# Spatial-shift token mixing in a GFNet + S-MLP block: eleven matmuls a block from packed transposes, with two neighbour copies

## The chip, the cores and the metric

The kernel runs on one core of one Trainium2 chip. The metric is the device time of one execution in microseconds (us); the table below gives the median of three runs and, beside it, the one execution that the profiler recorded.

## The reference

x has 2048 tokens of 448 features, w1 and w2 are 448x448, w3 is 448x1792, w4 is 1792x448; all are float32.

```python
x  = A_x;  xn = layernorm(x)
A  = irfft2(rfft2(xn) * (w_r + 1j * w_i))        # global filter branch
h  = gelu(layernorm(xn) @ w1)                    # token mixing of branch B
g0 = shift(h[:, 0:112], +1);   g1 = shift(h[:, 112:224], -1)      # by tokens, zeros at the ends
g2 = shift(h[:, 224:336], +2); g3 = shift(h[:, 336:448], -2)
x1 = xn + concat(g0, g1, g2, g3) @ w2
B  = x1 + gelu(layernorm(x1) @ w3) @ w4          # channel MLP
out = x + A + B
```

The part that the change touches is the token mixing: the product with w2 takes each quarter of h from another token.

## The kernel before, in words

**Precision.** Each float32 operand of a product is kept as two float16 tiles, a high half and a low half (what the high half leaves). A product is three passes: high x high, high x low, low x high. The weights are first scaled by a power of two that comes from their mean square (`squares`, `powers`, lines 238 to 257).

**Blocks of tokens.** Token 16a + b lies on partition a of block b, so the 2048 tokens are 16 blocks of 128 rows (`xb(b)`), and the neighbour of a token is the same partition of the neighbouring block, but for the ends: behind block 15 comes block 0, one partition further. The blocks are worked on in four groups of four, `GRP = [[14,15,0,1],[2,3,4,5],[6,7,8,9],[10,11,12,13]]`.

**First product** (`w1_in`, `w1_unit`, lines 408 to 441). Groups 0 to 2 are normalised, transposed on TensorE and split (L374, L378, L379), group 3 is transposed by DMA (`turn`, L842). Then each block makes eleven matmuls of 448 columns with w1 (L414). The first group's four blocks run side by side, pass by pass, in four PSUM banks. ScalarE applies the gelu in place (L433) and copies the high half (L434), VectorE makes the low half (L435); both lie in one of a few buffers `hs_buf` as 2 halves x 4 quarters x 128 columns (112 used). One DMA transpose a block (L438, on SP's queue) turns that into the eight 112-row tiles of `hT`.

**Token mixing** (`w2_tile`, L443 to L457). For each block b, quarter k is taken from the transposed tile of block b minus 1, plus 1, minus 2 or plus 2; at the ends the offset by one partition is one column of `hT` to the left or right, for which group 0's tiles have extra zero columns. Three passes of each of four quarters: twelve matmuls of 112 rows and 448 columns. VectorE adds the result into x (L456).

**After it.** `ln2` normalises x1, splits it and transposes it by DMA (L490) into `x2all`, which lies in the scratch tile `x2mem`. The channel MLP runs in pairs of blocks G (`front` L385 with w3, gelu and halves at L705 to L708, `back` L787 with w4). Its matmuls fill the gaps of the Fourier branch (L543, L601, L618, L646, L667, L688). w3 is loaded with x at the start (L213), its last part later (L216); the four pieces of w4 are loaded behind the transposes of groups 2 and 3 into `x2mem` (L228) and squared there (L242).

**What sets the order.** The Tile scheduler lays out each engine's instructions when the kernel is built, from the order of the code, priorities (`prio`) and the `behind(...)` marks (an instruction is placed behind another). On the chip each engine runs that list in order. SP issues nearly all DMAs of the kernel, in its own order, on one queue. TensorE begins with `WARM` = 28 matmuls on zeros (L817) while the first inputs are loaded.

Of the kernel before, what the change touches and what calls it, by code (L numbers as in the profile page):

```python
# [25 lines left out]
SHIFT = [1, -1, 2, -2]  # L26
WARM = 28
# [9 lines left out]
HS = 3  # L37
# [31 lines left out]
def constants():  # L69
# [20 lines left out]
    for c in range(NC):  # L90
        for j8, (k1, t) in enumerate(slots(c)):
            for j, (kr, s, base) in enumerate(rows(c)):
                if base != k1:
                    continue
                phi = tau * np.outer(np.arange(NB), kr + 128 * np.arange(16)) / S
# [28 lines left out]
def body(tc, nc, x, wf, w1, w2, w3, w4, c_g, c_n, c_small, out):  # L124
# [46 lines left out]

    def stage(name, n, side, dtype=F32):
        t = pw.tile([128, 1808], F32, tag=f"stage{side}", bufs=1, name=name)
        return (t if dtype is F32 else t.bitcast(dtype))[:, :n]
# [31 lines left out]
    SY.dma_start(w2s[:112], w2.rearrange("(k p) n -> p k n", p=112))  # L206
# [14 lines left out]
    x2mem = pw.tile([128, 9 * F], F16, name="x2mem")  # L221
    x2all = x2mem[:, 0:8 * F].rearrange("p (j t n) -> p j t n", j=4, t=7)
    w4raw = x2mem.bitcast(F32)[:, F:].rearrange("p (f n) -> p f n", f=14)
    w4v = w4.rearrange("(f p) n -> p f n", p=128)
    W4F = (0, 4, 8, 11, 14)

    def load_w4(i):
        SY.dma_start(w4raw[:, W4F[i]:W4F[i + 1]], w4v[:, W4F[i]:W4F[i + 1]])  # L228

    csm = pc.tile([128, 2 * (256 + 2 * DF + 452 + 128)], F16, name="csm")  # L230
# [162 lines left out]
    w2p = pr.tile([112, 2, 4, D], F16, name="w2p")  # L393
# [3 lines left out]

    def h_alloc(g):
        t = {0: 0, 1: 1, 2: 2, 3: 1}[g]
        hT[g] = pr.tile([128, 8, 512 if g else 592], F16, tag=f"h{t}", name=f"h{g}")  # L400
        if g == 0:
            P.memset(hT[g][:, :, 0:576].rearrange("p t (b a) -> p t b a", b=4)[:, :, :, 0:16], 0.0)
            P.memset(hT[g][:, :, 576:592], 0.0)

    def h_at(g, i):
        return 128 * i if g else 144 * i + 16
# [9 lines left out]

    hs_buf = [p1.tile([128, 2, 4, 128], F16, name=f"hs{i}") for i in range(HS)]
    for t in hs_buf:
        P.memset(t.rearrange("p i k n -> p (i k) n")[:, :, 112:], 0.0)

    for o in (0, 1024):
        hs_buf.append(x2mem[:, o:o + 1024].rearrange("p (i k n) -> p i k n", i=2, k=4))
        P.memset(hs_buf[-1].rearrange("p i k n -> p (i k) n")[:, :, 112:], 0.0)

    def w1_unit(g, i, pm=None):
        if pm is None:
            pm = bank(("tr" if g == 1 else "mm", "acc")[i // 2], f"pw1_{g}{i}")
            w1_in(g, [(i, pm)], range(4))
        c = CS[GRP[g][i]]
        pm = pm[:, :D]  # L430
        pv_ = pm.rearrange("p (k n) -> p k n", k=4)
        h = hs_buf[c % (HS if g == 3 else HS + 2)]
        A.activation(out=pm, in_=pm, func=AF.Gelu_apprx_tanh, scale=gsc[:, c:c + 1])  # L433
        u = A.activation(out=h[:, 0, :, 0:112], in_=pv_, func=AF.Copy, scale=h1)  # L434
        v = V.scalar_tensor_tensor(out=h[:, 1, :, 0:112], in0=pv_, scalar=h1, in1=h[:, 0, :, 0:112],  # L435
                                   op0=ALU.mult, op1=ALU.subtract)
        o = h_at(g, i)
        d = SY.dma_start_transpose(out=hT[g][:, :, o:o + 128], in_=h.rearrange("p i k n -> p (i k n)"))  # L438
        after[g, i] = u.ins, v.ins
        after["h", g, i] = (d.ins,)  # L440

    def w2_tile(b):
        pm = bank("sp", f"pw2_{b}")  # L443
        n = 0
        for k in (2, 0, 1, 3):
            src, o = b - SHIFT[k], 1
            if src < 0:
                src, o = src + NB, 0
            elif src >= NB:
                src, o = src - NB, 2  # L450
            g, i = WHERE[src]
            o += h_at(g, i) - 1
            for hi, wi in ((0, 0), (0, 1), (1, 0)):
                T.matmul(pm[:, :D], hT[g][:112, 4 * hi + k, o:o + 128], w2p[:, wi, k], start=n == 0, stop=n == 11)  # L454
                n += 1
        V.scalar_tensor_tensor(out=xb(b), in0=xb(b), scalar=cs[:, CS[b]:CS[b] + 1], in1=pm[:, :D],  # L456
                               op0=ALU.mult, op1=ALU.add)  # L457

    def ln2(bs, engines):
# [22 lines left out]
        for i in range(n):  # L482
# [7 lines left out]
            d = SY.dma_start_transpose(out=x2all[:, b // 4][:, :, 128 * (b % 4):128 * (b % 4) + 128], in_=h)  # L490
            after[f"b{b0}"] = u.ins, v.ins, d.ins

    def unscale(p, part):
        t = part.rearrange("p (b n) -> p b n", b=2)
        SY.dma_start(t, xv[:, 2 * p:2 * p + 2])
        return lambda: V.scalar_tensor_tensor(out=xt[p], in0=xt[p], scalar=p12, in1=t, op0=ALU.mult, op1=ALU.add)

    def finish(b):
        t = xb(b)
        if b < 2:  # L500
            t = row()[:, :D]
            SY.dma_start(t, xv[:, b])
            V.scalar_tensor_tensor(out=t, in0=xb(b), scalar=p12, in1=t, op0=ALU.mult, op1=ALU.add)
        SY.dma_start(ov[:, b], t)
# [6 lines left out]
    def do_fold(b0):  # L511
        X = pfd.tile([128, 2, D + 1], F32, tag="xf", bufs=3, name=f"xf{b0}")
        after["X", b0] = (SY.dma_start(X[:, :, 0:D], xv[:, b0:b0 + 2]).ins,)
# [181 lines left out]
    def front(G, fp, tag):  # L695
        tok = slice(256 * (G % 2), 256 * (G % 2) + 256)
        pm = bank(tag, f"pw3_{G}{fp}")
        for ff in range(2):
            f = 2 * fp + ff
            mlp_in(pm[:, 256 * ff:256 * ff + 256], w3p, slice(128 * f, 128 * f + 128), x2all[:, G // 2], tok)  # L700
# [66 lines left out]
    def back(G, fp):  # L767
# [10 lines left out]
        for i in range(2):  # L778
# [12 lines left out]
            if end:  # L791
                with prio(EVAC):
                    for r, to in parts:
                        V.scalar_tensor_tensor(out=xb(b)[:, r], in0=to, scalar=p34[:, min(G, 1):min(G, 1) + 1],  # L794
                                               in1=xb(b)[:, r], op0=ALU.mult, op1=ALU.add)
                        if G > 4:
                            SY.dma_start(ov[:, b, r], xb(b)[:, r])
# [51 lines left out]
    def w4_split(f):  # L849
        split_w(w4p[0][:, 0, f:f + 2], w4p[0][:, 1, f:f + 2], w4raw[:, f:f + 2], s4)  # L850
# [7 lines left out]
    h_alloc(0)  # L858
# [8 lines left out]
    for t in range(4):  # L867
        w1_in(0, list(enumerate(first)), [t])
    n1[0][0]()
    with behind("w1", 1):  # L870
        n1.append(norm1(1, [P, V, A, V]))
    with behind("w1", 3):
        squares(m2[:112], flat(w2s[:112]))
# [10 lines left out]
    n1[1][0]()  # L884
    with behind("a1"):
        w1_unit(0, 0, first[0])
        n1.append(norm1(2, [P, V, A, P]))
    with behind("a1"), behind("n", 2):
        for k in range(1, 4):
            w1_unit(0, k, first[k])  # L890
    with behind("na", 2):
        for k in range(4):
            split_w(w2p[:, 0, k], w2p[:, 1, k], w2s[:112, k], s2[:112], P)
    h_alloc(1)
# [3 lines left out]
    with behind("h", 1, 3):  # L898
        load_w3([3])
    n1[2][0]()  # L900
# [4 lines left out]
    h_alloc(2)  # L905
    for k in range(4):
        w1_unit(2, k)
    for k in range(4):
        with behind(*(("a2",), ("a2",), (2, 0), (2, 1))[k]):
            squares(m3[:, k:k + 1], w3raw[:, k])  # L910
    s3, r3 = powers(m3, 4, "3", "mm")
# [8 lines left out]
    with behind("t", 3), behind("h", 2, 3), behind("b0"):  # L920
        for i in range(4):
            load_w4(i)
    for b in range(4, 8):
        w2_tile(b)
        with behind(*PIN[b - 4]):
            w3_split(2 * b - 8)
            w3_split(2 * b - 7)
            for i in (2 * b - 10, 2 * b - 9):
                if i >= 0:
                    squares(m4[:, i:i + 1], flat(w4raw[:, 2 * i:2 * i + 2]), junk4)  # L930
    squares(m4[:, 6:7], flat(w4raw[:, 12:14]), junk4)
    ln2([2, 3], [A, P])
    h_alloc(3)
# [11 lines left out]
    for j in range(4):  # L945
        homes[j] = x2mem[:, F * j:F * j + F]
# [122 lines left out]
```

## Time and profile before

| | us |
|---|---|
| median of three runs (410.96 to 412.3) | 411.34 |
| the profiled execution, whole | 410.65 |
| its span, first to last instruction | 408.9 |
| TensorE matmuls busy in the span | 402.3 (98%) |
| VectorE busy | 330.7 (81%) |
| ScalarE busy | 256.5 (63%) |
| GpSimd busy | 95.3 (23%) |
| hardware DMA queue, share of 16 engines | 46.0% |

The durations and places used later are those of the profiled execution, counted from the start of its span. PE is TensorE's matmul, PEld its weight load, DVE VectorE, ACT ScalarE, POOL GpSimd, SP the engine that issues the DMAs. A line number (L454) is a line of the kernel before.

### The profile page before, as it was taken

The page shows a single profiled execution, that of the slowest core. Times are in us where ns is not written, and L with a number is a line of the kernel's source. Part 1 is how long each engine was busy: PE and PEld are TensorE (multiplying, and loading weights), DVE is VectorE, ACT ScalarE, POOL GpSimd, SP SyncE. Part 2 cuts the span into 40 slices and gives each one's busy share as a digit, 9 for nine tenths or more (in the row PEclk, how much of TensorE's full clock was granted, in tenths as well). Part 3 has the DMA queues.
Part 4 walks back from the last instruction along what each step waited for, and adds up shares of the span by engine and source line. Part 5 has one row for each costly group of instructions (what it writes and reads, how often), then busy time and mean ns, then how long its engine had stood idle before and what let it go on. Part 6 is the DMA issues. An engine that isn't in the chain of part 4 may idle for free.

```text
span 408.9 us, 8745 instructions
## 1 busy us (share of the span) xinstructions
PE 402.3 (98%) x3409; PEld 299.0 (73%) x3409; DVE 330.7 (81%) x686; ACT 256.5 (63%) x434; POOL 95.3 (23%) x172
## 2 busy tenths in 40 slices
PE   7999999999999999999999999999999999999996
PEld 3655555765668777777887887877777779998995
DVE  4888999898857678887798888955899989966645
ACT  4698879973758866556598888863453554453431
POOL 3877720101336748400012111110000000000000
PEclk9999999999999999999999999999999999999999
DMA  8959879914786456516255666500011022100101
GB/s 278 354 192 179 153 149 321 177 62 90 156 231 202 137 196 210 170 59 183 63 145 143 155 156 171 147 27 3 24 68 69 25 88 85 55 2 2 45 2 45
DMA packets 56168, 51.28 MB, mean 125 GB/s; under 512 B 37632, under 2 KB 50496, under 8 KB 56128
## 3 DMA queue, kind: packets, MB, share of 16 engines
q1 hardware_dynamic: 56128, 50.74, 46.0%
q8 instruction: 26, 0.43, 0.4%
q14 instruction: 14, 0.11, 0.1%
HBM read 38.28 MB, written 3.67 MB: 103 GB/s over the span
## 4 chain that ended last, share of the span: by engine, by line
PE 94%; DVE 3%; DMA 2%; POOL 0%; issue 0%; ACT 0%; SPq 0%; POOLq 0%
PE pw L385 33%; PE acc L787 23%; PE pw L454 9%; PE pw L414 6%; PE side L757 4%; PE acc L757 3%; PE pu L646 3%; PE ps L543 3%; PE pe L667 2%; PE pp L601 2%; PE px L618 2%; PE py L688 2%; DVE sta L293 1%; DMA xt<-x 1%; DMA h<-hs 1%; PE pta L374 1%
## 5 line engine op out<-in xcount | busy, mean ns | idle before, releaser
L385 PE MATMUL pw<-x2mem,w3p 128*128 128x256 f16 x1232 | 151.1, 273 | 0.0
L385 PEld LDWEIGHTS <-w3p 128*128 128x128 f16 x1232 | 119.2, 98 | 20.6
L787 PE MATMUL acc<-w4p,hf 128*128 128x448 f16 (+1 forms) x516 | 105.4, 348 | 0.0
L787 PEld LDWEIGHTS <-hf 128*128 128x128 f16 x516 | 49.8, 98 | 36.5
L705 ACT ACTIVATE pw<-pw,pe 128x512 f32<-128x512 f32 x42 | 27.5, 655 | 35.7 <-PE pw L385 35.7
L708 DVE SCALAR_TENSOR_TENSOR hf<-pw,h,hf 128x512 f16<-128x512 f32 x42 | 31.3, 748 | 14.5 <-ACT hf L707 14.4
L454 PE MATMUL pw<-w2p,h 112*128 112x448 f16 x192 | 39.9, 352 | 0.8 <-DMA h<-hs 0.8
L414 PE MATMUL pw<-w1p,xT 128*128 128x448 f16 x176 | 35.4, 352 | 0.0
L627 POOL TENSOR_TENSOR z<-te 128x450 f32<-128x450 f32 x16 | 15.7, 982 | 70.3 <-DVE te L625 70.3
L454 PEld LDWEIGHTS <-h 112*128 112x128 f16 x192 | 18.6, 98 | 17.2 <-DMA h<-hs 1.0
L707 ACT ACTIVATE hf<-pw,h 128x512 f16<-128x512 f32 x42 | 28.7, 686 | 1.0
L414 PEld LDWEIGHTS <-xT 128*128 128x128 f16 x176 | 16.9, 98 | 16.4 <-DVE xT L379 0.8
L723 ACT ACTIVATE hz<-g,h 128x896 f16<-128x896 f32 x14 | 14.6, 1044 | 22.3 <-DVE g L720 22.2
L757 PEld LDWEIGHTS <-hz 128*128 128x128 f16 x294 | 28.2, 98 | 0.4
L608 ACT ACTIVATE pf<-pp 64x450 f16<-64x450 f32 x32 | 17.4, 544 | 12.3 <-DVE pf L609 8.0
L609 DVE TENSOR_TENSOR pf<-pp,pf 64x450 f16<-64x450 f32 x32 | 19.9, 622 | 3.4 <-ACT pf L608 3.0
L724 DVE SCALAR_TENSOR_TENSOR hz<-g,h,hz 128x896 f16<-128x896 f32 x14 | 16.1, 1150 | 7.6 <-ACT hz L723 7.6
L623 ACT ACTIVATE te<-px 64x450 f32<-64x450 f32 x32 | 17.3, 542 | 1.2 <-PE px L618 0.6
L526 POOL TENSOR_TENSOR f<-xr 128x452 f32<-128x452 f32 x16 | 16.4, 1046 | 0.6
L717 ACT ACTIVATE g<-pw,pe 128x512 f32<-128x512 f32 x14 | 9.6, 684 | 10.2 <-PE pw L385 10.1
L794 DVE SCALAR_TENSOR_TENSOR xt<-acc,p,xt 128x448 f32<-128x448 f32 (+1 forms) x17 | 10.9, 654 | 6.2 <-PE acc L787 6.0
L523 POOL TENSOR_TENSOR xr<-xf 128x452 f32<-128x452 f32 x8 | 9.7, 1211 | 26.7 <-issue 20.3
(183 smaller groups left out, 705.7 us busy)
## 6 DMA issues: line engine op xcount, KB each, us to landing
wc<-wf SPq DMA_DIRECT2D x32, 225.0 KB, 3.8
wl<-wf SPq DMA_DIRECT2D x8, 450.0 KB, 4.1
xt<-x SPq DMA_DIRECT2D x8, 448.0 KB, 7.9
xf<-x SPq DMA_DIRECT2D x8, 448.0 KB, 3.6
loads<-x SPq DMA_DIRECT2D x7, 448.0 KB, 4.0
out<-xt SPq DMA_DIRECT2D x13, 224.0 KB, 1.9
w3raw<-w SPq DMA_DIRECT2D x3, 896.0 KB, 12.6
gn<-c_g SPq DMA_DIRECT2D x16, 128.0 KB, 3.1
```

The costliest lines, as they stand in the source:

```text
L385: T.matmul(ps_out, wp[:, wi + t, cols], xT[:, xi + t, tok], start=t == 0 and wi + xi == 0, stop=t == 3 and wi == 4)
L414: T.matmul(pm[:, :D], xTs[g][:, xi + t, 128 * i:128 * i + 128], w1p[:, wi + t], start=t == 0 and p == 0, stop=t == 3 and p == 2)
L454: T.matmul(pm[:, :D], hT[g][:112, 4 * hi + k, o:o + 128], w2p[:, wi, k], start=n == 0, stop=n == 11)
L526: P.tensor_tensor(out=f[:, :, k:k + 2].rearrange("p b s d -> p s b d"), in0=u[:, :, 0], in1=u[:, :, 1], op=op)
L608: A.activation(out=hi, in_=src, func=AF.Copy)
L609: V.tensor_tensor(out=lo, in0=src, in1=hi, op=ALU.subtract)
L623: A.activation(out=e[64 * h:64 * h + 64], in_=px_[64 - 64 * h:128 - 64 * h, :2 * DF], func=AF.Copy)
L705: A.activation(out=pm, in_=pm, func=AF.Gelu_apprx_tanh, scale=r3)
L707: i = A.activation(out=h[:, 0], in_=pm, func=AF.Copy, scale=h3)
L708: j = V.scalar_tensor_tensor(out=h[:, 1], in0=pm, scalar=h3, in1=h[:, 0], op0=ALU.mult, op1=ALU.subtract)
L757: m = T.matmul(to, h[:, hi, 128 * blk:128 * blk + 128], b[wi], start=new and n == 0, stop=n == 2 and (last if blk in (2, 5, 3, 0) else end ...
L787: m = T.matmul(to, h[:, hi, o:o + 128], w4p[0][:, wi, f, r], start=first and f % 2 == 0 and n == 0, stop=end and f % 2 == 1 and n == 2, sk ...
```

## The change

**Packed quarters.** Blocks are renumbered by two (`FIRST = 2`: block b holds the tokens 16a + (b + 2) mod 16), and w1's columns and w2's rows are put in the order of `TURN = [3, 1, 0, 2]` on the host. A unit of the first product no longer writes its quarters into a buffer of its own, but each quarter into the slot of the block that will use it: block c's quarters go to the slots of c - 2, c - 1, c + 1 and c + 2. A slot (in `x2mem`, now 10 F wide, 20 slots) is 448 high columns and 448 low columns side by side, without padding, and one DMA transpose makes seven full tiles of 128 rows of it instead of eight of 112. A slot is transposed when its last writer is done (`DONE`). The low half is two VectorE instructions of 224 columns.

**Eleven matmuls.** Tiles 0 to 2 are high, tile 3 is half high and half low, tiles 4 to 6 are low. w2's halves lie in eleven tiles `w2p`; two DMAs copy parts of the high half 64 partitions up or down for the tiles that begin in the middle (SBUF to SBUF, 64 rows of 2688 and of 3584 bytes).

**Neighbours over the end.** `wrap_on` copies the two slots that the first two blocks wrote for blocks 12 and 13 one partition down, `wrap_back` copies the two slots that the last two blocks wrote for blocks 14 and 15 one partition up: each one DMA of 127 rows of 3584 bytes from SBUF to SBUF on SP's queue. Behind the second, GpSimd copies three quarters (two for block 14, one for block 15) into their slots, and these are transposed. In SP's built order `wrap_on` stands ahead of the first slot's transpose, then come that transpose, the two copies of w2's halves and three more transposes; `wrap_back` stands behind the transposes of blocks 11 and 12, ahead of those of 14 and 15, the constants and eight transposes of `ln2`.

**First products.** For the last two of the four row tiles, the first group's blocks are finished one after the other; the gelu of its first two blocks is placed ahead of the copies of group 1's transposes, and GpSimd's refinement of the first scales behind its work on w1.

**w4.** Four of the 14 parts are loaded behind w3 at the start, six behind w3's last part, into a tile of their own; the other four later into `x2mem`. The squares are taken in that order.

**Else.** `WARM` is 24; x is loaded in the order of the groups; a scratch size is set at the build.

The diff, cut to its core:

```diff
-SHIFT = [1, -1, 2, -2]
-WARM = 28
+TURN = [3, 1, 0, 2]
+DONE = {c: [c - 2] for c in range(2, 12)} | {12: [10, 13], 13: [11, 12, 14, 15]}
+FIRST = 2
+WARM = 24
...
-        for b0 in sorted(GRP[g])[::2]:
-            SY.dma_start(xt[b0 // 2], xv[:, b0:b0 + 2])
+        for b0 in GRP[g][::2]:
+            SY.dma_start(xt[b0 // 2], xv[:, at_token(b0):at_token(b0) + 2])
...
+    load_w4(4, 4)
...
-    w2p = pr.tile([112, 2, 4, D], F16, name="w2p")
+    w2p = pr.tile([128, 11, D], F16, name="w2p")
...
+    def slot(b):
+        return x2mem[:, 896 * b + 3584:896 * b + 4480].rearrange("p (i n) -> p i n", i=2)
+
+    def slots_of(c, i):
+
+        t = slot(c - 2)[:, i]
+        return bass.AP(t.tensor, t.offset, [list(t.ap[0]), [3 * 896 + 224, 2], [896 + 112, 2], [1, 112]])
...
+    pairs = [x2mem[:, 896 * b + 3584:896 * b + 5376] for b in (-4, 12, 14)]
...
+    def wrap_on():
+        SY.dma_start(pairs[1][0:127], pairs[0][1:128])
+        P.memset(pairs[0][0:1], 0.0)
+
+    def wrap_back():
+        SY.dma_start(pairs[0][1:128], pairs[2][0:127])
+        for b, k in ((-2, slice(224, 448)), (-1, slice(336, 448))):
+            P.tensor_copy(out=slot(b)[:, :, k], in_=slot(b - 2)[:, :, k])
...
-        u = A.activation(out=h[:, 0, :, 0:112], in_=pv_, func=AF.Copy, scale=h1)
-        v = V.scalar_tensor_tensor(out=h[:, 1, :, 0:112], in0=pv_, scalar=h1, in1=h[:, 0, :, 0:112],
-                                   op0=ALU.mult, op1=ALU.subtract)
-        o = h_at(g, i)
-        d = SY.dma_start_transpose(out=hT[g][:, :, o:o + 128], in_=h.rearrange("p i k n -> p (i k n)"))
+        u = A.activation(out=h[0], in_=pv_, func=AF.Copy, scale=h1)
+        for k in range(2):
+            v = V.scalar_tensor_tensor(out=h[1][:, k], in0=pv_[:, k], scalar=h1, in1=h[0][:, k],
+                                       op0=ALU.mult, op1=ALU.subtract)
...
+        for b in DONE.get(GRP[g][i], ()):
+            if b == 14:
+                wrap_back()
...
+            d = SY.dma_start_transpose(out=hT[b // 4][:, :, 128 * (b % 4):128 * (b % 4) + 128],
+                                       in_=slot(b if b < 14 else b - 16).rearrange("p i n -> p (i n)"))
...
-            for hi, wi in ((0, 0), (0, 1), (1, 0)):
-                T.matmul(pm[:, :D], hT[g][:112, 4 * hi + k, o:o + 128], w2p[:, wi, k], start=n == 0, stop=n == 11)
-                n += 1
+        for n, (k, w) in enumerate([(k, w) for k in range(3) for w in (k, k + 7)] + [(3, 10)] + [(k, k) for k in (3, 4, 5, 6)]):
+            T.matmul(pm[:, :D], h[:, k], w2p[:, w], start=n == 0, stop=n == 10)
...
-    for t in range(4):
-        w1_in(0, list(enumerate(first)), [t])
-    n1[0][0]()
+    for t in range(2):
+        w1_in(0, list(enumerate(first)), [t])
+    for unit in enumerate(first):
+        w1_in(0, [unit], [2, 3])
+    with behind("w1", 3):
+        n1[0][0]()
...
+    for k in range(2):
+        w1_unit(0, k, first[k])
...
+    wrap_on()
...
+        SY.dma_start(w2p[64:128, 3:7], w2p[0:64, 0:4])
+        SY.dma_start(w2p[0:64, 4:7], w2p[64:128, 0:3])
...
         load_w3([3])
+        load_w4(8, 6)
...
-        for i in range(4):
-            load_w4(i)
+        load_w4(0, 4)
```

More of the change, by code (lines that the diff above doesn't have):

```diff
@@ L415, in w1_in @@
                                  start=t == 0 and p == 0, stop=t == 3 and p == 2)
[L417 to L423, printed above, removed]
+    def slot(b):
[4 more added lines that the diff above has]
+    pairs = [x2mem[:, 896 * b + 3584:896 * b + 5376] for b in (-4, 12, 14)]
+    for t in pairs[::2]:
+        P.memset(t, 0.0)
+    P.memset(pairs[1][96:128], 0.0)
+    def wrap_on():
[5 more added lines that the diff above has]
+            P.tensor_copy(out=slot(b)[:, :, k], in_=slot(b - 2)[:, :, k])
     def w1_unit(g, i, pm=None):
@@ L442, in w2_tile @@
+        for b in DONE.get(GRP[g][i], ()):
+            if b == 14:
+                wrap_back()
+            if b // 4 not in hT:
+                hT[b // 4] = pr.tile([128, 7, 512], F16, tag="h", bufs=2, name=f"h{b // 4}")
+            d = SY.dma_start_transpose(out=hT[b // 4][:, :, 128 * (b % 4):128 * (b % 4) + 128],
+                                       in_=slot(b if b < 14 else b - 16).rearrange("p i n -> p (i n)"))
+            after["h", g, i] = (d.ins,)
     def w2_tile(b):
         pm = bank("sp", f"pw2_{b}")
-        n = 0
@@ L884, in body @@
     n1[1][0]()
+    for k in range(2):
+        w1_unit(0, k, first[k])
     with behind("a1"):
-        w1_unit(0, 0, first[0])
         n1.append(norm1(2, [P, V, A, P]))
     with behind("a1"), behind("n", 2):
-        for k in range(1, 4):
+        for k in range(2, 4):
             w1_unit(0, k, first[k])
+    wrap_on()
     with behind("na", 2):
         for k in range(4):
-            split_w(w2p[:, 0, k], w2p[:, 1, k], w2s[:112, k], s2[:112], P)
-    h_alloc(1)
+            r = slice(0, 128 if k < 3 else 64)
+            split_w(w2p[r, k], w2p[r, 7 + k], w2s[r, k], s2[r], P)
+        SY.dma_start(w2p[64:128, 3:7], w2p[0:64, 0:4])
+        SY.dma_start(w2p[0:64, 4:7], w2p[64:128, 0:3])
     for k in range(4):
@@ L910, in body @@
             squares(m3[:, k:k + 1], w3raw[:, k])
+    for i in (2, 3):
+        with behind(2, 2):
+            squares(m4[:, i:i + 1], flat(w4raw(2 * i, 2)), junk4)
     s3, r3 = powers(m3, 4, "3", "mm")
```

81 lines of the change are left out of this document (33 added, 48 removed).

## The prediction

> **What bounds the kernel now.** I read the page first: busy times, the share of each line in the chain that ended last, then the costliest groups.
>
> ```profile
> span 408.9 us, 8745 instructions
> ...
> PE 402.3 (98%) x3409; PEld 299.0 (73%) x3409; DVE 330.7 (81%) x686; ACT 256.5 (63%) x434; POOL 95.3 (23%) x172
> ...
> L454 PE MATMUL pw<-w2p,h 112*128 112x448 f16 x192 | 39.9, 352 | 0.8 <-DMA h<-hs 0.8
> ```
>
> TensorE is busy for 402.3 of 408.9 us; the whole span holds some 6.6 us without a matmul. The token-mixing product (L454, twelve matmuls for each of 16 blocks) waited once, 0.8 us, for a transposed block. The profiled execution took 410.65 us, 1.75 more than its span; the median of the three runs is 411.34, 0.7 above it.
>
> Next, TensorE by stage, from the view of windows (us, then busy and count for PE, PEld, DVE, ACT, POOL, the granted clock, DMA share, GB/s):
>
> ```profile
> 35.00:60.00 25.00, 25.00 (x135) 12.97 (x134) 23.89 (x75) 19.32 (x30) 13.07 (x41) 1.00 0.88 159
> 60.00:95.00 35.00, 35.00 (x234) 22.62 (x233) 33.16 (x72) 29.40 (x48) 2.56 (x4) 1.00 0.68 171
> 95.00:121.00 26.00, 26.00 (x163) 15.69 (x161) 19.58 (x56) 15.03 (x24) 7.38 (x13) 1.00 0.76 164
> ```
>
> From 35 us on TensorE has no gap. DVE is nearly as full (33.16 of 35 us between 60 and 95), but off the path while TensorE has work queued. So two things can move the time: fewer matmuls, and new gaps. The timeline of TensorE around the first token-mixing product shows where a gap would come:
>
> ```profile
> 31.16 1.04 PE L374 MATMUL pta<-ident,xt 128*128 128x128 f32 x8
> 32.04 0.35 PE L454 MATMUL pw<-w2p,h 112*128 112x448 f16 x1
> 32.23 0.60 PE L374 MATMUL pta<-ident,xt 128*128 128x128 f32 x4
> 33.62 0.36 PE L454 MATMUL pw<-w2p,h 112*128 112x448 f16 x1 [0.79 <-DMA h<-hs]
> 33.82 0.60 PE L374 MATMUL pta<-ident,xt 128*64 128x128 f32 x4
> 34.42 2.05 PE L454 MATMUL pw<-w2p,h 112*128 112x448 f16 x10
> ...
> 40.88 6.22 PE L414 MATMUL pw<-w1p,xT 128*128 128x448 f16 x32
> 46.94 0.35 PE L454 MATMUL pw<-w2p,h 112*128 112x448 f16 x1
> ```
>
> My landmark is 46.94 us, the end of the first product of group 2 (L414): up to there both kernels do the same TensorE work, but for two blocks of token mixing.
>
> **The change part by part.** *Matmuls.* The chain of waits, in order of time, gives the pitch of one:
>
> ```profile
> 96.43 2.27 PE pw L454 x12
> ```
>
> 2.27 / 12 = 0.189 us (the 352 ns of the group is a latency, overlapped). Eleven instead of twelve, in 16 blocks: 16 x 0.189 = **-3.03 us**, all on the path, since TensorE has no gap there. From the second block pair of the channel MLP on, at about 120 us, the order of instructions on every engine is unchanged, so nothing is added or hidden behind that point.
>
> *The first neighbour copy.* It moves 127 rows of 3,584 bytes, 455,168 bytes, from SBUF to SBUF on SP's queue, and stands ahead of every token-mixing transpose there. Before, the quarters were taken from four transposed tiles and no such copy exists, so I bound it. What one DMA engine moves comes from the windows:
>
> ```profile
> 4.00:6.00 2.00, 2.00 (x10) 0.88 (x9) 0.56 (x2) 0.00 (x0) 0.00 (x0) 1.00 1.01 368
> 20.44:24.50 4.06, 4.06 (x29) 2.50 (x26) 2.69 (x6) 3.38 (x7) 2.79 (x14) 1.00 1.03 408
> 24.50:28.00 3.50, 3.50 (x20) 1.83 (x20) 3.50 (x11) 3.50 (x8) 3.06 (x6) 1.00 0.06 19
> 29.00:46.00 17.00, 16.21 (x93) 8.88 (x91) 15.21 (x41) 13.95 (x23) 12.25 (x31) 1.00 0.98 177
> ```
>
> Sixteen engines at a share of 1.03 move 408 GB/s: 24.8 GB/s each. Spread over all sixteen the copy takes 455,168 / 408e3 = 1.1 us; on a single one, 455,168 / 24.8e3 = 18.4 us. These are the ends. The transfers of the trace have 128, 112 or 64 rows, all of which can be dealt out equally to sixteen engines, and none has another count. 127 is prime: it can be dealt out equally to one engine alone. I take the single engine, **18.4 us**.
>
> The Trainium skill says the same of such a copy ("DMA: Bandwidth & Descriptors", section "Why a DMA increments its semaphore by 16 and not by 1"): the number of engines is the largest one up to 16 that divides the leading size of both sides, and 127 partitions is its example for one engine. No run here shows it yet; by the page the copy is a slow one, and by the nearest rows (128 rows) a fast one.
>
> Does it hold up what is issued behind it? The view of DMA issues (count, KB each, median us from issue to landing):
>
> ```profile
> w1s<-w SPq DMA_DIRECT2D x2, 112.0 KB, 5.9
> out<-xt SPq DMA_DIRECT2D x2, 112.0 KB, 1.8
> ```
>
> The same 112 KB take 1.8 us on an empty queue and 5.9 us behind the first loads: a transfer waits for what was queued ahead. A transpose uses all sixteen engines (share 0.98 between 29 and 46 us, mostly transposes), so it is done only when the engine of the copy is free again.
>
> So: the first loads keep the queue full to 24.5 us (share 1.03, then 0.06). The change adds four of w4's 14 parts to them, 917,504 bytes / 408e3 = 2.2 us: 26.7. The copy can be issued before that, since its two blocks are evacuated first. 26.7 + 18.4 = 45.1. The first packed block, 229,376 bytes at the transposes' 177 GB/s: 1.3 us, 46.4. Only then can its product start, and TensorE's order is fixed: what stands behind cannot pass. TensorE reaches it at about 33.4 (31.16 plus 2.2 us of 16 transposes), so it idles some 13 us. Behind it, to the landmark: 22 token-mixing and 44 L414 matmuls, 66 x 0.189 = 12.5.
>
> Coming from idle costs too. The kernel's start shows it:
>
> ```profile
> 1.22 7.53 PE L817 MATMUL wps<-wsrc 128*128 128x512 f16 x28 [1.22 <-DVE wsrc L187]
> ```
>
> 28 matmuls in 7.53 us, where ten take 2.00 us in the window from 4 to 6, after the ramp, and 512 columns at the pitch of 448 take 0.216, so 28 take 6.0: the ramp costs 1.5 us. The skill ("TensorE: Matmul & The Clock Gate", Part 1) lets the clock fall to half after an idle window of 3.4 us; the slow first matmuls agree, no row of before shows an idle TensorE in mid-kernel. Between 0 and 1.5 I take 1.5, as 13 us is longer than any gap here.
>
> Landmark after: 46.4 + 12.5 + 1.5 = 60.4, against 46.94: **+13.5**, the first two blocks' saving included. The other 14 blocks save 14 x 0.189 = 2.65. Net **+10.8 us**.
>
> *The second copy*, same size, goes out behind the transposes of the last units. SP's timeline before:
>
> ```profile
> 73.74 6.62 SPq L438 DMA_TRANSPOSE h<-hs  x4
> 80.42 0.57 SPq L937 DMA_DIRECT2D csm<-c_small  x1
> 95.15 13.57 SPq L490 DMA_TRANSPOSE x2mem<-y  x8
> ```
>
> Shifted by 13.5 these end near 94, or 88 where the last two go behind the copy. 88 + 18.4 = 106; two small POOL copies (nearest row below, 0.64 us each) and one transpose (3.2 us median) make it 111. Block 14's product stood at 96.43 and comes 13.5 - 12 x 0.189 = 11 us later: 107 to 108, or a little later as the static order has more pieces of the channel MLP ahead of it. Loss 0 to 3 us; I take 0, as DVE and ACT also lag, and keep 3 for the range. Queued behind on SP are the constants and eight transposes, which before had 15 us of slack (80.42 to 95.15).
>
> ```profile
> 74.49 0.64 POOL L478 TENSOR_SCALAR y<-xt,nm 128x448 f32<-128x448 f32 x1
> ...
> L435 DVE SCALAR_TENSOR_TENSOR hs<-pw,h,hs 128x448 f16<-128x448 f32 x8 | 5.3, 675 | 0.8 <-ACT hs L434 0.8
> L488 DVE SCALAR_TENSOR_TENSOR y<-y,vs 128x384 f16<-128x384 f32 x2 | 1.2, 612 | 0.0
> L486 DVE SCALAR_TENSOR_TENSOR y<-y,vs 128x64 f16<-128x64 f32 x2 | 0.5, 265 | 0.0
> ```
>
> *Small edits.* Each unit's low half is two DVE instructions of 224 instead of one of 448: 612 + 265 = 877 ns for 448 columns in two, against 675, so +0.2 us for each of 16. Those ahead of 46 us lie in the idle time above; the others beside TensorE (if that cover is gone, 8 x 0.2 = 1.6). Four warm-up matmuls less, the gradual ending of the first products, the order of ACT and POOL, the memsets, the order of loading x: all lie ahead of 33.4 us and are covered by the 13 us. w2's two half copies (64 rows, divisible by 16) queue behind the first block, about 1 us, while twelve other matmuls run (2.3 us). The rest of w4, loaded earlier, feeds sums that had no wait on the path. I cost all these at 0.
>
> **The rivals.** *Spread copy (ends faster).* If the copy is dealt over sixteen engines it is gone by 28 us. The first block is then released by DVE: before, the fifth unit's low half ended at about 32.1; plus 3.2 us issue to landing is 35.3, some 2 us after TensorE arrives. Landmark 35.3 + 12.5 = 47.8, +0.9; less 2.65: -1.8, 409.5 us. Against it: 127. It decides from three engines on (18.4 / 3 = 6.1 us, done by 33).
>
> *Slow copy that others pass.* If the copy sits on one engine but this engine serves the transposes alternately, the first block costs about 1.3 us more and the following ones as much again: -1.8 + 2.5, 412 us. Against it: the 5.9 us of the w1s row.
>
> *Nothing of the gain, DVE bound*: DVE's extra halves uncovered, -1.8 + 1.6 = 411 us; I count it with the first two.
>
> **How the numbers follow.** One engine, others held: 0.80; 408.9 + 10.8 = 419.7 us span, 421.5 with what lies around it, 422.1 on the median's footing: I say 422. Its own range is 417.5 (no ramp, copy and loads 3 us shorter together) to 427.5 (22.8 GB/s as in the 4-to-6 window, +1.6, second copy +3, and a us of DVE lag). Spread: 0.13, 408 to 411. Passed: 0.07, 411 to 414. The range 411.5 to 427.5 leaves the spread case and the tails out. A measurement can tell 0.3% (1.2 us) from no change: faster 0.12, same 0.05, slower 0.83.
>
> **What would show it.** Right: TensorE idle for over 10 us before the first packed product, ended by the DMA of h; the copy's landing some 18 us after 27; low DMA share between 28 and 45; token mixing at 176 matmuls of 0.189. Wrong: the first copy landing within 4 us, or transposes landing during it; then the landmark lies near 48. A second wait before block 14 is the copy's twin.

## The result, and the profile after

The changed kernel takes **441.66 us** (median of 4 runs, 440.9 to 442.36) against 411.15 (4 runs, 410.73 to 412.3) on the same chip: ratio **1.0737** (95% interval 1.0707 to 1.0767), 30.5 us slower. The forecast was 422.0, and 427.5 at most. The profiled execution took 442.03 us.

The page after, with the lines that answer to those of before, and TensorE's waits (line, releaser: us in total, times, longest):

```profile
span 439.9 us, 8719 instructions
...
PE 407.5 (93%) x3389; PEld 299.6 (68%) x3389; DVE 333.6 (76%) x702; ACT 255.6 (58%) x434; POOL 100.1 (23%) x173
...
L469 PE MATMUL pw<-w2p,h 128*128 128x448 f16 x176 | 38.6, 375 | 20.3 <-DMA h<-x2mem 20.3
```

```profile
PE pw L469 <- DMA h<-x2mem: 20.3, 3, 11.2
PE acc L801 <- ACT hf L721: 2.9, 1, 2.9
PE pm L259 <- DVE pt L257: 2.3, 1, 2.3
```

Token mixing (L469 now) has the forecast 176 matmuls. But TensorE is without a matmul for 439.9 - 407.5 = 32.4 us instead of 6.6 (+25.8), and its busy time has grown by 5.2 us, though 16 matmuls (3.0 us) and four of the warm-up are gone. The two make up the 31.0 us of the span. The mean of an L469 matmul is 375 ns instead of 352: part of the remaining work ran slowly. TensorE's timeline has the places:

```profile
34.08 1.91 PE L384 MATMUL pta<-ident,xt 128*128 128x128 f32 x16
47.20 2.42 PE L469 MATMUL pw<-w2p,h 128*128 128x448 f16 x6 [11.21 <-DMA h<-x2mem]
...
61.99 4.33 PE L469 MATMUL pw<-w2p,h 128*128 128x448 f16 x22
...
113.08 0.92 PE L801 MATMUL acc<-w4p,hf 128*128 128x448 f16 x4
122.84 4.28 PE L469 MATMUL pw<-w2p,h 128*128 128x448 f16 x11 [8.84 <-DMA h<-x2mem]
...
142.97 0.55 PE L801 MATMUL acc<-w4p,hf 128*128 128x448 f16 x2 [2.91 <-ACT hf L721]
```

Three gaps: 11.21 us before the first packed block, 8.84 before block 14, and 2.91 in the channel MLP. Behind them matmuls take up to twice their time: block 14's eleven need 4.28 us, a block at full clock 2.24. The windows (us, busy and count of PE, PEld, DVE, ACT, POOL, granted clock, DMA share, GB/s) show the copies themselves and a dropped clock:

```profile
36.00:44.00 8.00, 0.00 (x0) 0.00 (x0) 6.21 (x12) 5.95 (x9) 4.04 (x14) 0.64 0.06 26
102.00:116.00 14.00, 12.00 (x70) 6.63 (x68) 13.28 (x37) 3.97 (x6) 0.00 (x0) 1.00 0.06 26
```

```profile
95.00:121.00 26.00, 19.00 (x113) 10.85 (x111) 20.02 (x56) 10.16 (x14) 1.06 (x3) 0.92 0.21 48
```

A share of 0.06 is one engine of sixteen, moving 26 GB/s, with nothing beside it. In the trace's packets each row of 3,584 bytes takes 0.142 us; 127 of them make 18.0 us. The packets also show how the transpose behind the copy is held: 504 of its 896 packets of 256 bytes (229,376 / 256) start between 34.38 and 35.99 us, then none until 45.72, just behind the copy's last packet at 45.71. Where the stretch from 95 to 121 us had 26.00 of 26 us of matmuls before, it has 19.00. SP's timeline (start, length of the issues, line, what, count) tells who stood behind:

```profile
25.21 0.74 SPq L434 DMA_DIRECT2D x2mem<-x2mem  x1
33.10 7.78 SPq L461 DMA_TRANSPOSE h<-x2mem  x1
...
91.75 6.62 SPq L461 DMA_TRANSPOSE h<-x2mem  x5
98.50 0.68 SPq L438 DMA_DIRECT2D x2mem<-x2mem  x1
119.76 3.00 SPq L461 DMA_TRANSPOSE h<-x2mem  x2
122.81 0.58 SPq L956 DMA_DIRECT2D csm<-c_small  x1
124.61 17.82 SPq L504 DMA_TRANSPOSE x2mem<-y  x8
```

The second copy is issued at 98.50 and its two followers at 119.76; `ln2`'s eight transposes, which began at 95.15 before, begin at 124.61. The hold is not the same at both copies. At the first, the transposes are issued and land late. At the second, the transposes of blocks 14 and 15 need the copied rows themselves, by way of GpSimd's copies, and SP does not issue them before these are made; `ln2`'s eight stand behind them in SP's list. SP's longest wait (line, releaser, us in total, times, longest) is this one, ended at 119.76 amid GpSimd's copies:

```profile
SPq L461 <- POOL nm L481: 21.0, 1, 21.0
```

What waits shows on GpSimd (the copies of three quarters) and on ScalarE:

```profile
119.17 0.87 POOL L440 COPY x2mem<-x2mem 128x448 f16<-128x448 f16 x2 [24.93 <-DMA x2mem<-x2mem]
```

```profile
129.79 0.67 ACT L490 ACTIVATE y<-xt,nm 128x448 f32<-128x448 f32 x1 [22.97 <-DMA x2mem<-y]
```

ScalarE stands still for 22.97 us for the buffer of `y` that these transposes had not yet read. Its next gelu (L719) is behind that instruction, and VectorE, which waits for the gelu's halves, stands for 18.27 us. From that backlog comes the third gap of TensorE (`acc` waits for `hf`): the `hf` of 142.25 us stands on ScalarE behind another part of `ln2` (L490 at 141.67), which waited 4.28 us for GpSimd's `nm`, and `nm` for VectorE's statistics.

### The profile page after: what moved, and what is told of

Its sections match the earlier page's. It is cut to its first block, busy times and chain, and to the rows that moved or that the text cites. A ratio compares the mean times of both kernels' runs of the same rounds, so it can differ in the third digit from the quotient of the medians.

```text
span 439.9 us, 8719 instructions
## 1 busy us (share of the span) xinstructions
PE 407.5 (93%) x3389; PEld 299.6 (68%) x3389; DVE 333.6 (76%) x702; ACT 255.6 (58%) x434; POOL 100.1 (23%) x173
## 4 chain that ended last, share of the span: by engine, by line
PE 56%; DMA 2%; issue 1%; DVE 1%; POOL 0%; SPq 0%
PE pw L395 22%; PE acc L801 15%; PE side L771 4%; PE acc L771 3%; PE pu L660 2%; PE pp L615 2%; PE pe L681 2%; PE px L632 2%; PE py L702 2%; DMA wl<-wf 2%; PE ps L557 1%; DVE wm L270 0%; POOL xr L538 0%; POOL f L540 0%; DVE y L562 0%
## 5 line engine op out<-in xcount | busy, mean ns | idle before, releaser
L801 PE MATMUL acc<-w4p,hf 128*128 128x448 f16 (+1 forms) x516 | 107.6, 352 | 3.2 <-ACT hf L721 2.9
L469 PE MATMUL pw<-w2p,h 128*128 128x448 f16 x176 | 38.6, 375 | 20.3 <-DMA h<-x2mem 20.3
L722 DVE SCALAR_TENSOR_TENSOR hf<-pw,h,hf 128x512 f16<-128x512 f32 x42 | 31.3, 745 | 28.9 <-ACT hf L721 28.7
L469 PEld LDWEIGHTS <-h 128*128 128x128 f16 x176 | 17.8, 102 | 38.3 <-DMA h<-x2mem 21.5
L719 ACT ACTIVATE pw<-pw,pe 128x512 f32<-128x512 f32 x42 | 27.4, 653 | 28.1 <-PE pw L395 27.7
L415 PE MATMUL pw<-w1p,xT 128*128 128x448 f16 x176 | 36.6, 363 | 1.1 <-DVE xT L389 0.6
L415 PEld LDWEIGHTS <-xT 128*128 128x128 f16 x176 | 17.4, 101 | 19.0 <-issue 2.3
L622 ACT ACTIVATE pf<-pp 64x450 f16<-64x450 f32 x32 | 17.4, 543 | 12.3 <-DVE pf L623 8.0
L490 ACT ACTIVATE y<-xt,nm 128x448 f32<-128x448 f32 x8 | 5.3, 668 | 32.2 <-DMA x2mem<-y 24.9
L450 ACT ACTIVATE pw<-pw,gsc 128x448 f32<-128x448 f32 x16 | 9.4, 598 | 18.6 <-POOL nm L481 15.7
L470 DVE SCALAR_TENSOR_TENSOR xt<-xt,cs,pw 128x448 f32<-128x448 f32 x16 | 10.8, 673 | 11.9 <-PE pw L469 11.9
L548 DVE TENSOR_TENSOR xh<-f,xh 128x452 f16<-128x452 f32 x16 | 12.6, 822 | 7.4 <-ACT xh L547 7.4
```

The lines of the kernel that those rows point to most:

```text
L415: T.matmul(pm[:, :D], xTs[g][:, xi + t, 128 * i:128 * i + 128], w1p[:, wi + t], start=t == 0 and p == 0, stop=t == 3 and p == 2)
L469: T.matmul(pm[:, :D], h[:, k], w2p[:, w], start=n == 0, stop=n == 10)
L622: A.activation(out=hi, in_=src, func=AF.Copy)
L722: j = V.scalar_tensor_tensor(out=h[:, 1], in0=pm, scalar=h3, in1=h[:, 0], op0=ALU.mult, op1=ALU.subtract)
L801: m = T.matmul(to, h[:, hi, o:o + 128], w4p[0][:, wi, f, r], start=first and f % 2 == 0 and n == 0, stop=end and f % 2 == 1 and n == 2, sk ...
```

## The experiments

My theory was the forecast's, with its second term corrected: **a copy of 127 rows goes on one DMA engine, and every transfer behind it waits for that engine; both copies cost so.** The rivals: the queue and not the engine holds the transposes; the packing's order costs the time, not the copies; copies within the chip's memory are slow whatever their rows. All ratios are against runs of the kernel before on the same chip (medians of 410.84 to 411.15 us; 411.15 for the changed kernel, 410.84 for the four kernels below it in the table).

**Undoing the copies' row count, one and both.** Each copy as two DMAs of 112 and 15 rows, both the same bytes:

```diff
-        SY.dma_start(pairs[1][0:127], pairs[0][1:128])
+        SY.dma_start(pairs[1][0:112], pairs[0][1:113])
+        SY.dma_start(pairs[1][112:127], pairs[0][113:128])
...
-        SY.dma_start(pairs[0][1:128], pairs[2][0:127])
+        SY.dma_start(pairs[0][1:113], pairs[2][0:112])
+        SY.dma_start(pairs[0][113:128], pairs[2][112:127])
```

Both:

> Both neighbour copies are made as two DMAs, of 112 rows and of 15 rows; nothing else is changed. Theory (a 127-row DMA sits on one DMA engine for 18 us and holds up every transpose queued behind it; everything else of the change is about as priced): TensorE's waits for h of 11.2 and 8.8 us and the three half-clock stretches behind them vanish, time 409 to 413 us, the upper part because the half-clock stretch at 10.9 to 14.4 us is now uncovered. Rival (the packed slots themselves wait: five units, then DVE halves, then one transpose): the waits stay above 5 us each, time above 425.

The first only:

> Only the first neighbour copy is made as 112 and 15 rows; the second stays one DMA of 127 rows. Theory: the gap of 11.2 us before the first packed product goes, the second copy keeps its 18 us and the wait before block 14 stays at 8 to 10 us with its half-clock ramp: 424 to 428 us. Rival (the two copies' losses are one loss, the second wait only follows from the delay of the first): the second wait falls under 3 us, time under 416.

The second only:

> Only the second neighbour copy is made as 112 and 15 rows; the first stays one DMA of 127 rows. Theory: the gap of 11.2 us stays with its ramp, the wait before block 14 and what follows it goes: 422 to 426 us, which is what the prediction gave for a first copy alone (422). Rival (the 17 us that the prediction lacks have another origin than the second copy): over 432 us.

And both, with `WARM = 28` again:

> Both copies as 112 and 15 rows, and 28 warm-up matmuls as before instead of 24. Theory: with 24, TensorE's idle time ahead of the first power (2.3 us instead of 1.2) lets the clock fall to half for 3.4 us; with 28 this stretch goes and the time is 1 to 1.7 us below the run with 24, about 408.5 to 410, faster than the kernel before. Rival (the clock's fall does not hang on these four matmuls, or is covered by the wait for the first packed block): the same time within 0.5 us.

| kernel | us (median) | ratio to before (95%) |
|---|---|---|
| changed | 441.66 | 1.0737 (1.0707 to 1.0767) |
| first copy split | 429.18 | 1.0439 (1.0424 to 1.0454) |
| second copy split | 424.89 | 1.0342 (1.0329 to 1.0355) |
| both split | 412.97 | 1.0053 (1.0034 to 1.0071) |
| both split, WARM 28 | 412.09 | 1.0031 (1.0019 to 1.0043) |

Undoing the first copy gives 12.5 us (11.9 where the second is split already), the second 16.8 (16.2 where the first is), both 28.7 of the 30.5: nearly additive. Two of the four ranges were missed: the first split came out 1.2 us above its 428, and the kernel with `WARM = 28`, which I had expected at 408.5 to 410, faster than the kernel before, is not faster. TensorE's waits with the first split, and with the second split, show one gap each:

```profile
PE pw L470 <- DMA h<-x2mem: 9.9, 5, 8.9
PE acc L802 <- ACT hf L722: 3.8, 2, 3.4
```

```profile
PE pw L470 <- DMA h<-x2mem: 11.2, 2, 10.9
...
PE acc L802 <- ACT hf L722: 0.4, 1, 0.4
```

The wait for `hf` goes with the second copy. From the changed kernel to the one with the second copy split the span falls by 439.9 - 422.4 = 17.5 us: 9.1 of it is the wait for h, 2.5 the wait for `hf`, 4.3 TensorE's busy time (407.5 to 403.2, slow matmuls), 1.4 the wait for `pt` at the start, which varies (below), so that part of the 16.8 us may not be the copy's.

**The copy alone, in the kernel before.** A copy of two unused stretches that nobody reads, ahead of the first transposes, once of 127 rows and once of 128:

```diff
+    spare = x2mem[:, 2 * F:4 * F]
+    P.memset(spare, 0.0)
+    with behind("w1", 1):
+        SY.dma_start(spare[0:127, 0:F], spare[1:128, F:2 * F])
```

For 128 rows the last line has `spare[0:128, 0:F], spare[0:128, F:2 * F]`.

> The kernel before, with one copy of 127 rows x 3,584 bytes between two stretches of x2mem that are not in use yet, issued on SP just ahead of the first transposes of h; nobody reads it and nothing is left out. Theory 1 (a copy of 127 rows holds the queue for some 18 us): the first transposes of h land some 18 us later, TensorE waits 9 to 13 us for them, time 420 to 425 us. Theory 2 (the loss comes from what the packing does to the order of the work, and a copy by itself costs nothing): 411 to 412.5 us.

> As the run with 127 rows, but the copy has 128 rows (1 per cent more bytes). Theory 1 (the row count sets the number of engines): the copy is done in 1 to 2 us on sixteen engines, time 411 to 412.5 us, against 420 to 425 with 127 rows. Theory 2 (a copy between two places of the memory on chip is slow or blocks the queue whatever its rows): as with 127 rows.

127 rows: 424.52 us, ratio 1.032 (1.0301 to 1.0339). 128 rows: 410.86 us, ratio 0.9994 (0.9982 to 1.0006). One row more, and 13.7 us are gone. (The copy of 128 rows is also not shifted by a partition; the split copies above are, and are harmless, so the shift is not what costs.) The first waits of TensorE for h and the window from 34 to 42 us, 127 rows and then 128:

```profile
44.09 0.55 PE L454 MATMUL pw<-w2p,h 112*128 112x448 f16 x1 [11.74 <-DMA h<-hs]
```

```profile
34.00:42.00 8.00, 0.00 (x0) 0.00 (x0) 0.00 (x0) 0.00 (x0) 4.26 (x16) 0.66 0.06 26
```

```profile
33.62 0.36 PE L454 MATMUL pw<-w2p,h 112*128 112x448 f16 x1 [0.80 <-DMA h<-hs]
```

```profile
34.00:42.00 8.00, 8.00 (x44) 4.03 (x43) 7.94 (x20) 5.80 (x9) 4.13 (x16) 1.00 1.16 175
```

The kernel before has nothing of the packing, so such a gap doesn't need the packing's order; and a copy within the chip's memory of 128 rows costs nothing. Both rivals fall.

**How many engines.** 124 + 3 rows instead of 127:

```diff
-        SY.dma_start(pairs[1][0:127], pairs[0][1:128])
+        SY.dma_start(pairs[1][0:124], pairs[0][1:125])
+        SY.dma_start(pairs[1][124:127], pairs[0][125:128])
...
-        SY.dma_start(pairs[0][1:128], pairs[2][0:127])
+        SY.dma_start(pairs[0][1:125], pairs[2][0:124])
+        SY.dma_start(pairs[0][125:128], pairs[2][124:127])
```

> Both copies as 124 + 3 rows instead of 127; nothing is left out. Theory 1 (the number of DMA engines is the largest number up to 16 that divides the rows): 124 rows go on four engines and 3 rows on three, so a copy of 31 packets of 140 ns on each takes 4.3 us and a DMA share near 0.25 instead of 0.06. The wait for h before the first packed product then shrinks from 11.2 us to 0 to 3 us, the one before block 14 from 8.8 to under 1; time 412 to 416 us (the split into 112 + 15 rows gave 413.0). Theory 2 (whatever sixteen does not divide goes on one engine): 124 rows take 17.4 us, DMA share 0.06, time 436 to 442 us.

417.14 us, ratio 1.0154 (1.013 to 1.0178), 1 us above the expected range and far from the rival's. Between 28 and 30 us, with little but the copy in flight:

```profile
28.00:30.00 2.00, 2.00 (x12) 1.03 (x11) 1.31 (x8) 1.78 (x4) 1.81 (x11) 1.00 0.25 100
```

Share 0.25, four engines, 100 GB/s: four times the 26 above. 124 = 4 x 31. The Trainium skill's rule, quoted in the prediction, gives 4 for 124, 1 for 127 and 16 for 112 and 128. The traces agree on 4 and 1; that it is sixteen for 112 and 128 was not read off, but the rows of a copy as 112 + 15 all start within 2.4 to 4.4 us.

The microsecond that I missed, and the 4 us to the split of 112 + 15, lie at the second copy: ScalarE still waits 11.68 us for `ln2`'s transposes (22.97 in the changed kernel), and TensorE's longest wait is again the one for `hf`, 2.75 us at 115 us.

**Another queue.** Both copies from ScalarE's queue:

```diff
-        SY.dma_start(pairs[1][0:127], pairs[0][1:128])
+        A.dma_start(pairs[1][0:127], pairs[0][1:128])
...
-        SY.dma_start(pairs[0][1:128], pairs[2][0:127])
+        A.dma_start(pairs[0][1:128], pairs[2][0:127])
```

> The two copies of 127 rows are issued from ACT's DMA queue instead of SP's; nothing is left out. Both theories have the copy itself on one engine for 18 us or more. Theory 1 (the transposes are held because they stand behind the copy in the same queue): from another queue the engine serves both in turn, each transpose lands a little later instead of 18 us later, the wait for h before the first packed product falls from 11.2 us to under 6, time 413 to 428 us; what waits for the copied rows themselves still waits. Theory 2 (the packed blocks wait for the copied rows or for the engine, whatever the queue): wait of 10 to 13 us again, time 436 to 444 us.

442.87 us, ratio 1.0786 (1.075 to 1.0822): no better than on SP. TensorE waits 12.2 us before the first packed product and 12.5 us later on. So a queue of its own does not help. (The first wait shows that; block 14, behind the second, needs the copied rows whatever the queue.) But this kernel does not look the same while it waits:

```profile
36.00:44.00 8.00, 0.00 (x0) 0.00 (x0) 5.14 (x10) 4.85 (x7) 3.25 (x13) 0.57 1.14 51
```

All engines count as busy (1.14) and move 51 GB/s; in the run with 128 rows the same share moved 175. The transposes' packets of 256 bytes take 155 ns here (median of those that start between 36 and 40 us) and 18 ns once the copy is over: about one row of the copy (140) and their own time. So they seem to pass one for one in turn with its rows, and the transpose's other packets keep step; that reading rests on the packet times alone. Serving in turn, which the rival of the slow copy had at about 1.3 us for the first block and as much for the following ones, is thus as dear as waiting. The Trainium skill ("DMA: Bandwidth & Descriptors", section "Issuing engines are not separate DMA queues") says that transfers of different issuers run on the same sixteen engines and interleave there; the trace agrees.

**GpSimd as issuer.** The same edit with `P.dma_start`:

> The two copies of 127 rows are issued by GpSimd instead of SP; nothing is left out. Theory 1 (GpSimd writes the descriptors itself and deals the rows out over the engines): the copy is done in a few us, DMA share well over 0.06, time 412.5 to 416 us. Theory 2 (127 rows go to one engine whoever issues them): 18 us at a share of 0.06 and time 438 to 445 us. Theory 3 (they are spread, but GpSimd's time to issue delays its own work): 416 to 422 us.

413.9 us, ratio 1.0088 (1.0066 to 1.011), as with both copies split (412.97). The view of DMA issues and the window of the first copy:

```profile
x2mem<-x2mem POOLq DMA_DIRECT2D x2, 444.5 KB, 5.1
```

```profile
26.00:30.00 4.00, 4.00 (x22) 1.97 (x21) 3.80 (x15) 1.44 (x4) 3.73 (x10) 1.00 0.73 222
```

127 rows from GpSimd land in 5.1 us instead of about 20. The packets of these copies have 7,168 bytes, 63 of them and one of 3,588 each time. So the row count decides for SP's and ScalarE's transfers here, not for GpSimd's. The Trainium skill names such an exception for some copies that GpSimd issues, in the section that the prediction cites, and this run agrees.

**The first copy behind the first four transposes:**

```diff
-    wrap_on()
...
     T1(2)
     with behind("h", 1, 3):
+        wrap_on()
         load_w3([3])
```

> The first copy (127 rows) is issued behind the first four transposes of h and the two copies of w2's halves, ahead of the last part of w3; the second copy is unchanged; nothing is left out. Theory 1 (the copy holds what is queued behind it, and only that): the wait for h before the first packed product falls from 11.2 us to under 2, the engine is held from about 38 to 56 us instead, and the fifth block's transpose is late: a wait for h of 2 to 7 us where TensorE had none; the second copy's loss stays; time 430 to 438 us (429.2 with the first copy split, 441.7 with it in its place). Theory 2 (the copy costs what it costs wherever it stands): 439 to 443 us.

447.36 us, ratio 1.089 (1.0869 to 1.091): slower than in its old place, against my range of 430 to 438. The first gap is gone, as expected, and a larger one stands before the fifth block:

```profile
36.27 1.31 PE L469 MATMUL pw<-w2p,h 128*128 128x448 f16 x6 [0.16 <-DMA h<-x2mem]
...
71.99 3.54 PE L469 MATMUL pw<-w2p,h 128*128 128x448 f16 x9 [18.46 <-DMA h<-x2mem]
```

The copy is issued at 40.45 us and its last packet is at 64.95, 24.5 us later, where it was 20.5 in the old place (25.21 to 45.71). From 44 to 50 us it moves 13 to 15 rows in 2 us; from 50 to 58, while the loads of w3 and w4 behind it run, 7 or 8. So loads do not stand still behind the copy, and they slow it; the fifth transpose, issued at 50.44, waits for its end. "What is behind is held" holds for the transposes alone; my price of 2 to 7 us left out that slowing and a transpose needed earlier than I thought.

**What is left when both copies are split.** The kernel before with `WARM = 24`, and the split kernel with 28 and the first group's units placed as before:

```diff
-WARM = 28
+WARM = 24
```

> The kernel before with 24 warm-up matmuls instead of 28; nothing is left out. Theory 1 (the longer idle time ahead of the first transposes lets the clock fall, as with 24 in the changed kernel): a stretch at half clock of some 3 us after 10 us, time 411.8 to 412.8 us. Theory 2 (the warm-up only fills idle time): 410.8 to 411.4 us, no such stretch.

```diff
-WARM = 24
+WARM = 28
...
-    for k in range(2):
-        w1_unit(0, k, first[k])
     with behind("a1"):
+        w1_unit(0, 0, first[0])
         n1.append(norm1(2, [P, V, A, P]))
     with behind("a1"), behind("n", 2):
-        for k in range(2, 4):
+        for k in range(1, 4):
             w1_unit(0, k, first[k])
```

(and both copies as 112 + 15)

> The changed kernel with both copies as 112 + 15 rows, 28 warm-up matmuls, and the gelu and halves of the first group's blocks placed as in the kernel before (one block ahead of the third group's normalisation, three behind it); nothing is left out. Theory 1 (the placement of the first group's units delays the copies of the next transposes, which makes the small waits for xT and the late first landmark): those waits go, time 410.6 to 411.6 us, against 412.1 without this edit. Theory 2 (the first packed block is late for its two more writers anyway): the wait for h before it grows to 1 to 3 us, time 412 to 414 us.

`WARM = 24` alone: 411.06 us, ratio 1.0011 (1.0 to 1.0023), no half clock, so theory 1 is not borne out there. The other: 411.37 us, ratio 1.0014 (1.0002 to 1.0027), in the range of its first theory, but the waits that this theory had going are there, and it is not faster than before. The steps from 412.97 (both split) to 412.09 (`WARM` 28) and to 411.37 are smaller than the spread of these runs, and their intervals overlap: they are not shown to be gains. The spans of this kernel and of the one before are both 408.9 us, although this one has 16 matmuls less. Its timeline of TensorE:

```profile
1.22 9.12 PE L833 MATMUL wps<-wsrc 128*128 128x512 f16 x28 [1.22 <-DVE wsrc L191]
...
34.74 1.14 PE L415 MATMUL pw<-w1p,xT 128*128 128x448 f16 x4 [0.89 <-DVE xT L389]
36.88 1.12 PE L471 MATMUL pw<-w2p,h 128*128 128x448 f16 x5 [1.01 <-DMA h<-x2mem]
```

The first packed product starts at 36.88 us, where before a first quarter could start at 32.04. Between 30 and 60 us TensorE loses 0.89 + 1.01 + 0.68 = 2.6 us in waits against 0.8 before: 1.8 of the 3.0 us saved. The warm-up takes 1.6 us more in this execution (9.12 against 7.53), most of it in place of the wait behind it. What releases the first waits is VectorE (`xT`, and the low halves that the transpose needs). That these waits are the whole of the missing 3 us was not isolated.

## Why the prediction was wrong, point by point

- **TensorE bounds; 16 matmuls of 0.189 us go.** Right for the matmuls. TensorE's busy time with the copies harmless (from GpSimd) is 400.1 us, 2.2 below the 402.3 of before. But none of it reached the end of a run: with the second copy alone split, the span behind the landmark is 361.9 us (422.4 - 60.53) as before (408.9 - 46.94), where I had taken off 2.65. TensorE is busy 1.8 us less there and waits 1.8 us more, in pieces of up to 0.86 us. "TensorE has no gap there" was read from the kernel before.
- **The first copy, one engine, 18.4 us, +12.5 against a spread copy (422.0 - 409.5).** Right: one engine, 127 x 0.142 = 18.0 us, and undoing it gives 11.9 to 12.5. The first packed product started at 47.20 (forecast 46.4) and the landmark at 61.99 (60.4): 0.8 us for the copy and the loads ahead of it, the other 0.8 for the return of the clock, which cost 2.3 and not the 1.5 of the start: TensorE ran at half clock from 47.20 to 51.88. That the 12.5 is met so closely is in part luck, since the other end moved as well: with the copy split the landmark is at 49.01, not at 47.8. And the 5.9 us of the w1s row, taken as a sign that transfers wait for what is ahead, did not decide against a rival in which transfers pass in turn: from ScalarE's queue they seem to, and it was no faster.
- **The second copy, "Loss 0 to 3 us; I take 0".** This is the step that failed: **16.8 us** by undoing it, 16.2 where the first copy was split already. Its mechanism was named (the copy's twin); three sizes were off. It was issued at 98.50 instead of 88 (74.5 and the shift of 13.5). With the first copy split it is issued at 85.88, 11.4 us behind that 74.5: it stands behind the last units, whose slots it copies, and behind five transposes that end 5.4 us later than the four of before; I had taken off 6 us as if two of the four were out of its way. The 12.6 us of the first copy come on top. Block 14 was wanted at 114.0 instead of 107 to 108, which gave back 6.5 of it. And the product started at 122.84, not at 111: 8.84 us of wait where I had 3 to 4.
- **"DVE and ACT also lag" and "15 us of slack" as cover.** Wrong: what stands behind the copy on SP was itself on the way to the end. `ln2`'s transposes began 29.5 us later than before (17.4 later than at 107.24 with the second copy split), ScalarE stood for 22.97 us, and TensorE waited 2.91 us more.
- **The ramp.** I counted one. There were two more, behind the gaps of 8.84 and 2.91 us; they are the larger part of the 4.3 us of busy time that go with the second copy.
- **Small edits at 0, covered by the 13 us.** In the changed kernel they were under that cover. Without it (both copies split) the kernel is 2.1 us slower than before, where the spread rival had it 1.8 faster. With `WARM` at 28 it is 0.9 less, with the first units in their old place another 0.7, neither clear of the spread; what is missing for the most part is the saving itself (above).

Of the 19.7 us between 422.0 and 441.66, then, 16.8 go with the second copy. The other 2.9 are still there in the kernel with the second copy split (424.89), which is the case that my sum describes: its landmark is at 60.53 (forecast 60.4), and what is off comes behind it, where the saving of 2.65 stayed out. The sign, the place of the first gap and the engine count were right; the range failed by the second copy, a term that was sized from where things stood before the change.

## What to carry to other kernels

Count the rows of each DMA between partitions: shifting by one partition makes 127, and here that was 18 us on one engine, where 128 rows cost the kernel nothing, and it stopped every transpose behind it; with 112 + 15 rows, or GpSimd as issuer, the kernel came within 2.1 and 3.0 us of the one before. If one such transfer sits on the path, price its twins with the same care, from where they will be issued after the first delay, and ask of each thing that is queued behind whom it feeds. A saving in matmuls only counts if the producers (here VectorE's halves before a transpose) are ready as early as before.

## What was not expected of the hardware

The granted clock does not follow from the length of a gap alone. In the changed kernel it fell after a wait of 2.30 us near the start; in the kernel with GpSimd's copies a wait of 2.30 us, from 54.65 to 56.95, passed without a fall. In the clock records of each trace the changes lie whole multiples of 3.41 us apart, so I cut both kernels into these stretches, the first two lines for the changed kernel and the last two for GpSimd's copies:

```profile
7.51:10.92 3.41, 1.11 (x9) 0.65 (x7) 2.05 (x8) 2.29 (x7) 1.10 (x2) 1.00 1.00 317
10.92:14.33 3.41, 3.41 (x17) 2.75 (x15) 2.88 (x8) 3.05 (x7) 1.27 (x2) 0.50 1.06 311
```

```profile
53.09:56.51 3.42, 1.56 (x9) 0.59 (x6) 3.42 (x9) 3.42 (x7) 2.68 (x9) 1.00 0.86 163
56.51:59.92 3.41, 2.98 (x17) 1.70 (x18) 3.38 (x20) 2.70 (x6) 0.43 (x2) 1.00 0.95 179
```

The first wait lies in one stretch, 2.30 us idle, and the next stretch is at half clock. The second wait lies across a border, 1.86 us on one side and 0.43 on the other. Counted like this over all 14 profiles, each of the 17 stretches at full clock with 1.96 us or more without a matmul was followed by half clock, and none with 1.87 us or less. The clock came back only behind stretches with at most 0.59 us idle, and TensorE, once resumed, ran at half clock for 2.8 to 6.1 us behind the gaps of over 8 us.

The half clock near 11 us shows in the profiles with the long wait (1.96 to 2.33 us: changed, first split, both split, first copy moved) and not in those with 0.94 to 1.62 (second split, 124 + 3, GpSimd). All of these have 24 warm-up matmuls, whose time varied from 6.65 to 7.86 us, and the wait with it, so one profile each doesn't tie it to the edit. The Trainium skill ("TensorE: Matmul & The Clock Gate", Part 1) has the clock fall after an idle window of about 3.4 us; here 1.96 us idle in a stretch of 3.41 were enough.
